# A fused attention and mixture-of-experts kernel: the order of the slots' scatters, the place of one flag product, and the engine that writes the last tile

## The chip, the core and the metric

The kernel runs on one core of one Trainium2 chip. The metric is device time in microseconds (us): the median of the runs of one launch. TensorE is written PE here, with PEld for its weight loads; DVE is VectorE, ACT is ScalarE, POOL is GpSimd, SP is the queue that issues most transfers.

## The reference: what is computed

Windowed attention over q, k and v of shape 4 x 8 x 768 x 64 (batch, heads, tokens, width), then a router and eight experts over the 3072 rows of 512 that the attention gives:

```python
scores = scale * np.matmul(q, k.transpose(0, 1, 3, 2))
rel = pos[:, None] - pos[None, :]
is_global = pos[None, :] < int(n_global)
is_local = (rel >= 0) & (rel < int(n_local))
...
a = np.exp(scores)
a = a / (np.sum(a, axis=-1, keepdims=True) + 1e-09)
...
xn = x / (np.linalg.norm(x, axis=-1, keepdims=True) + 1e-06)
en = expert_emb / (np.linalg.norm(expert_emb, axis=-1, keepdims=True) + 1e-06)
logits = xn @ en.T / tau
expert_idx = np.argmax(logits, axis=1)
...
for e in range(E):
    mask = expert_idx == e
    h = np.maximum(x[mask] @ w1[e], 0.0)
    out[mask] = gate_w[mask, None] * (h @ w2[e])
```

With n_global = 8 and n_local = 96 each token attends to 96 tokens behind it and to the first eight. An expert multiplies its tokens by a 512 x 1024 and a 1024 x 512 matrix, all in float32.

## The kernel before, in words

**Attention** (`window_attention`, L377) works in 32 steps over groups of four heads, the first 24 for three batches one after the other and the last eight for the fourth. A step scores two blocks of 96 queries (`score`, L480), exponentiates them on ACT (`grow`, L486), multiplies them by a table of weights on DVE (`weigh`, L493), and multiplies the blocks of the step before by v (`attend`, L509 and L519). In the same steps the halves of a batch that are finished go through routing (`half_turns`, `half_router`): turning (L582, L550, L568), the division by the softmax sums on DVE (`store_x`, L591) with the square sum on ACT (L596), and the generator `choose` (L192), which is advanced one piece at a time. For the last two batches a half has three row blocks, and its router comes in the third turn (`hf.count` is 2); for the others a whole batch is chosen, one turn later.

`choose` gives each token its expert and its slot in a list in memory. Its pieces: the highest score and its expert on DVE (L203 to L211); then, when it is sent a bank, counting products on PE (L217, L220) and the root, a power on POOL (L224); then the new counts on DVE (L228, L230); then the scale of the logits from the root (DVE L234 to L236), the exponential (ACT L237) and the slot (L246). Each block's `scatter` (a reciprocal on DVE, L256, and an indirect DMA that POOL issues, L257) is put on the list `k.later`. `scatter_later` (L296) takes one, two or three blocks off it in each step (L789); the DMA is told to wait for the step's last score product (`scored`). All scatters must have landed before the first expert's slots are read (L976), and then its first 256 rows are gathered (L986) and run through its first matrix while attention ends (L663, L671).

**The experts** (L1688 to L1742). For each, tokens are gathered by POOL, turned, and multiplied by the first matrix by a seven-product scheme (`first_by_seven`, L1296 and L1308) in one of several arms of a Switch, each for a number of tokens. The second matrix takes whole tiles (L1229, L1231) and odd parts (L1242, L1244) in the arm, and the first two tiles by another seven-product scheme, `Pair` (L1085): sums of the weights and of the hidden values on DVE (L1040 to L1043, L1065 to L1068), products on PE (L1102), copies and scalings on ACT (L1128, L1132, L1139, L1154), sums on DVE (L1107, L1114). `Pair.fourth` writes a quarter of the first tile through ACT (L1148). `Pair.end` writes the last quarter in `rest` (L1160), which is issued in the next expert, or at the end of the program for the last one. The scatters of finished rows are issued by POOL (L1248).

**Flags.** `good` holds whether all softmax sums are in range (`check_sums`, L607), `fits` whether the two numbers fit the window. `flag_leftover` (L1514), issued inside expert 2 on the list `ahead`, multiplies the two (L1519, DVE), adds over partitions with a one-column product (L1520, PE) and makes a flag (L1521 to L1528). The program's end branches on it (L1542) to a slow path that isn't taken here.

**What sets the order.** In attention, PE, ACT, DVE and SP run in the order in which the program names the instructions; POOL's order there is chosen by the framework's scheduler. In the experts all five engines run in program order.

Of the kernel before, what the change touches and what calls it, by code (L numbers as in the profile page):

```python
# [12 lines left out]
ALU = mybir.AluOpType  # L13
# [282 lines left out]
def scatter_later(k, n, behind=None):  # L296

    for scatter, t in k.later[:n]:
        scatter(t, behind)
    del k.later[:n]  # L300
# [76 lines left out]
def window_attention(k, ctx):  # L377
# [375 lines left out]
    waiting, active = [], []  # L753
    weights = [(0, i) for i in range(PIECES)]
    for s, (g, p) in enumerate(steps):
        if s % 8 == 0:
            before = t if s else None
            pair = groups[s // 4 : s // 4 + 2]
            t = new_batch(g.b)
            t.groups = pair  # L760
            for x in pair:
                x.batch = t
        ahead = s // 4 + 2
        if ahead < len(groups):
            if s % 4 == 0:
                open_group(groups[ahead])
            load_part(groups[ahead], s % 4)
        if s == len(steps) - 5:
            early.close()
            k.w.append(new_weights(k, k.second_weights()))  # L770
            weights.extend((1, i) for i in range(PIECES))

        def weights_part(n=1):
            for _ in range(n):
                if s >= 11 and weights:
                    e, i = weights.pop(0)
                    load_weights_part(k, e, k.w[e], i)

        if s == 5:
            nc.sync.dma_start(k.x_dram[k.ZR : k.ZR + 1, :].rearrange("o (p c) -> (o p) c", p=P), k.zrow[:])  # L780
            empty_slots(k)

        us = g.units[2 * p : 2 * p + 2]
        for u in us:
            scored = score(u)
        grow(us[0], 0)
        grow(us[0], 1)
        weigh(us[0])
        scatter_later(k, 1 if s < len(steps) - 8 else 2 if s < len(steps) - 3 else 3, scored)  # L789
        grow(us[1], 0)  # L790
        todo = [(x.pairs[a], i) for x, a, i in turns[s]]
        if todo:
            turn(*todo.pop(0))
        grow(us[1], 1)
        for x in todo:
            turn(*x)
        if s == 2:
            next(table)
        if 1 <= s <= 3:
            emb.send(bank() if s == 3 else None)  # L800
        if waiting and (s >= 8 * (B - 1) or all(hf.phase >= 3 for hf in active)):
            active.append(start_half(*waiting.pop(0)))
        if s == len(steps) - 1:
            weigh(us[1])
        for hf in active:
            half_turns(hf)
        if s == len(steps) - 1:
            first_gathers()
        ready = s > 8 * (B - 1) - 2 and steps[s - 1][0].m == 1 and steps[s - 1][1] % 2
        if s < len(steps) - 1 and not ready:  # L810
            weigh(us[1])
        weights_part()
        for hf in active:
            if hf.router and hf.phase == hf.count:
                next(hf.router)
        if s > 0:
            q, qp = steps[s - 1]
            attend(q, qp, s < len(steps) - 10)
            if q.m == 1 and qp % 2:
                waiting.append((prev, qp // 2))  # L820
        if ready:
            weigh(us[1])
        for hf in active:
            if hf.phase == 0:
                score_experts(hf, bank())
            half_router(hf)
            hf.phase += 1
        active = [hf for hf in active if hf.phase < (hf.count + 2 if hf.router else 3)]
        if s == len(steps) - 3:
            scatter_later(k, len(k.later))  # L830
            first_rows()
        weights_part()
        prev = t
# [24 lines left out]
    scatter_later(k, len(k.later))  # L858
    check_sums(before)
    check_sums(t)  # L860
    for f in range(1, k.NF):
        first_product(f)

# [221 lines left out]
class Pair:  # L1085


    def __init__(self, k, rows, a, left, w2, sums):
        self.k, self.ids, self.a, self.left, self.sums = k, rows[1], a, left, sums
        self.gate = [rows[0][:, i, 2:3] for i in range(2)]  # L1090
        self.b = [[w2[:, 4 * i : 4 * i + 4, j * 256 : (j + 1) * 256] for j in range(2)] for i in range(2)]
        tmp = k.tp.tile([P, 5, 256], F32, name="ptmp", tag="ptmp")
        self.p1, self.p5, self.u2, self.u3, self.u3g = (tmp[:, i] for i in range(5))
        self.u2g = k.late.tile([P, 256], F32, name="u2g", tag="u2g")[:]
        self.y = [k.yp.tile([P, k.DM], F32, name="y", tag="y") for _ in range(2)]
# [49 lines left out]

    def fourth(self):
        self.product(self.m, self.a[0][1], self.b[1][0], True)
        self.k.nc.scalar.mul(self.part(0, 0), self.m, self.gate[0])  # L1148

    def end(self, ps):  # L1150

# [187 lines left out]
def expert(k, now, coming, widths, unfinished):  # L1339


    tc = k.tc
    w1, w2 = now.w
    hT = new_hidden(k)
    if coming:
        coming.xT = new_turned(k)

    def between(f):
        at = {1: (0,), 2: (1,), 3: (2,), 4: (3,)} if now.e else {5: (0,), 6: (1, 2), 7: (3,)}
        for j in at.get(f, ()) if coming else ():  # L1350
            turn_row(k, coming.rows, coming.xT, j, k.nc.scalar.copy)

    a = [[hT[:, 4 * j : 4 * j + 4, i * P : (i + 1) * P] for j in range(2)] for i in range(2)]
    now.sums, spare = weight_sums(k, w2)
    left, making = hidden_sums(k, a)
    more, ahead = [], []
    if coming:
        coming.token_sums, more = token_sums(k, coming.xT)
        if now.e:
            coming.first_sums, ahead = first_sums(k, coming.w[0])  # L1360
    spare = [spare[:2], spare[2:], ahead[:1], ahead[1:2], more[:2], []]
    if now.e == 1:
        spare[2:6] = [], ahead[:1], ahead[1:2] + more[:1], more[1:2]
    tiles = range(2 if now.e else 1, CAP // P)
    ps = None if now.e else k.work0.tile([P, k.DM], F32, name="work", tag="work")
    k.order = list(range(4, 8)) + list(range(4)) if now.e else list(range(8))
    steps = widths_of(now.e)
    for arm in tc.Switch(now.width.index, len(steps), hint=now.width.hint):
        w = steps[arm]
        if now.e:  # L1370
            first_by_seven(k, now, hT, w, between, list(spare))
            for make in making:
                make()
        else:
            first_by_eight(k, now.xT, w1, hT, w, between)
        for size in (32, 64):
            if w % (2 * size) >= size:
                part_in_arm(k, now, hT, w2, w // (2 * size) * 2 * size, size)
        for j in tiles:
            if j < w // P:  # L1380
                second_in_arm(k, now, hT, w2, j)
        if ps:
            second(k, ps, hT, w2, range(k.NF // 2))

    def scatters():
        for j in tiles:
            scatter_rows(k, now.y[:, j - 1, :], now.tile_ids[:, j : j + 1])
        for size in (64, 32):
            scatter_rows(k, now.y_part[size][:], now.parts[size][0], P // size)

    def choose_next():
        if coming:
            give_hint(k, coming.e, widths[coming.e])

    out = [scatters]
    if now.e:
        pair = Pair(k, now.rows, a, left, w2, now.sums)
        choose_next()
        out += unfinished.pop()()
        number = [lambda: widths.append(take_width(k, now.e + 2))] if now.e + 2 < k.E else []  # L1400
        if now.e == k.E - 2:
            number.append(lambda: load_flag(k))
        if now.e == 2:
            ahead.append(lambda: flag_leftover(k))
        pair.begin(spare=(more[2:], number + ahead[2:3], ahead[3:]))
        ps = k.work0.tile([P, k.DM], F32, name="work", tag="work")
        unfinished.append(pair.end(ps[:, 0:256]))
        out.append(pair.scatter(1))
    else:
        choose_next()  # L1410
        widths.append(take_width(k, 2))
        out += unfinished.pop()()
        for make in more:
            make()
        second(k, ps, hT, w2, range(k.NF // 2, k.NF))
        unfinished.append(lambda: end_second(k, now.rows, ps))
    return out
# [96 lines left out]
def flag_leftover(k):  # L1514

    nc = k.nc
    k.flags = flags = k.const.tile([P, 2], F32, name="flags")
    ps = k.work.tile([P, 512], F32, name="work", tag="work")
    nc.vector.tensor_tensor(out=k.good[:], in0=k.good[:], in1=k.fits[:], op=ALU.mult)  # L1519
    nc.tensor.matmul(ps[:, 0:1], lhsT=k.ones[:], rhs=k.good[:], start=True, stop=True)  # L1520
    nc.vector.tensor_scalar(out=flags[:, 0:1], in0=ps[:, 0:1], scalar1=float(P), scalar2=None,  # L1521
                            op0=ALU.is_lt)
# [251 lines left out]
```

## Time and profile before

| what | value |
|---|---|
| median of 3 runs | 529.67 us (523.33 to 529.82) |
| the profiled execution's own time | 530.46 us |
| its span, first to last instruction | 528.70 us |
| mean granted clock of PE | 0.988 |
| PE busy | 504.3 us (95%) |
| PEld busy | 415.2 us (79%) |
| DVE busy | 302.6 us (57%) |
| ACT busy | 198.0 us (37%) |
| POOL busy | 151.1 us (29%) |
| moved by DMA | 76.32 MB, 144 GB/s in the mean |

A line of the timeline gives the start and the duration in us, the engine, the line of the kernel, the operation, the tile written and the tiles read, and in brackets how long the engine stood idle before it and what ended that. A row of the stages gives a stretch, the busy time of PE, PEld, DVE, ACT and POOL in it with the number of instructions, the granted clock of PE as a share, the busy share of the DMA engines, and GB/s. In the 40-slice rows each digit is a tenth.

### The profile page before, as it was taken

The numbers are of one execution on the slowest core, as the hardware profiler recorded it, in microseconds if no ns is written. First come the engines' busy times: TensorE is split into PE (matmuls) and PEld (weight loads), VectorE is DVE, ScalarE is ACT, GpSimd is POOL, SyncE is SP. The second block draws the span as 40 slices with busy tenths as digits, with TensorE's granted clock in tenths as the row PEclk, the third lists the DMA queues.
The fourth block names the chain that finished last, engine by engine and source line by source line (L and its number), as shares of the span: only waits on it lengthen the run. The fifth ranks groups of instructions, "written<-read, shape, count | busy, mean of one in ns | idle before, by whom it ended". The sixth has DMA issues, their size and how long they took to land. (4 is left out here: it accounts for less than half of the span.)

```text
span 528.7 us, 13699 instructions
## 1 busy us (share of the span) xinstructions
PE 504.3 (95%) x5606; PEld 415.2 (79%) x5606; DVE 302.6 (57%) x601; ACT 198.0 (37%) x494; POOL 151.1 (29%) x169
## 2 busy tenths in 40 slices
PE   8999999999988999999989998999999999999995
PEld 7777787877765787859878757989989789859964
DVE  5646677766784573755745605675746645615531
ACT  4867766767654321302312312322322222312211
POOL 4222121151453234354240013344053050013022
PEclk9999999999998799999999999999999999999999
DMA  8989998999533234827683016548056064001001
GB/s 161 203 184 177 233 231 184 217 218 215 103 102 112 90 83 97 261 65 263 215 283 125 1 37 230 217 148 282 28 207 246 3 221 163 1 12 69 0 22 66
DMA packets 111421, 76.32 MB, mean 144 GB/s; under 512 B 87077, under 2 KB 95269, under 8 KB 111281
## 3 DMA queue, kind: packets, MB, share of 16 engines
q1 hardware_dynamic: 102769, 59.00, 42.6%
q0 software_dynamic: 6912, 15.26, 8.7%
q8 instruction: 63, 1.03, 0.9%
q14 instruction: 77, 0.63, 0.4%
q10 hardware_dynamic: 1600, 0.39, 0.3%
HBM read 61.66 MB, written 17.16 MB: 149 GB/s over the span
## 5 line engine op out<-in xcount | busy, mean ns | idle before, releaser
L493 DVE TENSOR_TENSOR ex<-ex,table 126x768 f32<-126x768 f32 x64 | 61.2, 961 | 44.9 <-ACT ex L486 44.0
L1308 DVE TENSOR_TENSOR hT<-big,hT 128x320 f32<-128x320 f32 (+4 forms) x70 | 39.4, 566 | 49.8 <-PE big L1296 48.4
L1248 POOL DMA_INDIRECT out_dram<-y_arm,tids x17 | 17.1, 1004 | 168.0 <-ACT y_arm L1231 121.7
L486 ACT ACTIVATE ex<-pa 126x384 f32<-126x384 f32 (+1 forms) x128 | 53.4, 476 | 21.9 <-PE pa L480 19.7
L1296 PE MATMUL big<-xT,w1t 128*128 128x160 f32 (+4 forms) x336 | 59.4, 330 | 1.7 <-issue 1.7
L1296 PEld LDWEIGHTS big<-xT,w1t 128*128 128x128 f32 x336 | 54.2, 190 | 4.4 <-issue 2.5
L509 PE MATMUL od<-ex,v 126*64 126x192 f32 (+1 forms) x576 | 49.8, 322 | 0.0
L986 POOL DMA_INDIRECT xg<-x_dram,idss x32 | 33.9, 1058 | 44.6 <-PE big L1296 22.9
L509 PEld LDWEIGHTS od<-ex,v 126*64 126x64 f32 x576 | 36.9, 145 | 8.6 <-issue 3.7
L480 PE MATMUL pa<-qT,kT 64*32 64x128 f32 (+3 forms) x2048 | 40.6, 268 | 2.6 <-issue 2.4
L480 PEld LDWEIGHTS pa<-qT,kT 64*32 64x32 f32 (+1 forms) x2048 | 30.9, 107 | 14.8 <-issue 11.9
L257 POOL DMA_INDIRECT meta<-mt,slot x24 | 27.7, 1154 | 44.9 <-DVE rd L553 21.1
L1296 PE MATMUL big<-xsum,fsum 128*128 128x160 f32 (+4 forms) x224 | 39.6, 330 | 0.0
L1015 ACT COPY xT<-work 128x256 f32<-128x256 f32 x56 | 18.0, 376 | 56.7 <-PE work L1012 55.3
L1296 PEld LDWEIGHTS big<-xsum,fsum 128*128 128x128 f32 x224 | 36.1, 190 | 1.1
L1229 PE MATMUL work<-w2t,hT 128*128 128x512 f32 x80 | 35.1, 593 | 0.0
L1102 PE MATMUL big<-wsum,hsum 128*128 128x256 f32 x136 | 31.1, 380 | 1.0 <-issue 0.5
L430 POOL COPY v<-v 30x896 f32<-30x896 f32 (+1 forms) x15 | 17.8, 1197 | 49.0 <-DMA v<-in_v_dram 29.4
L1310 ACT ACTIVATE hT<-hT 128x320 f32<-128x320 f32 (+4 forms) x42 | 21.6, 533 | 25.5 <-DVE hT L1308 25.3
L1102 PEld LDWEIGHTS big<-wsum,hsum 128*128 128x128 f32 x136 | 25.7, 190 | 5.6 <-issue 1.3
L1229 PEld LDWEIGHTS work<-w2t,hT 128*128 128x128 f32 x80 | 15.1, 190 | 17.7 <-issue 17.6
L1107 DVE TENSOR_TENSOR ptmp<-big,ptmp 128x256 f32<-128x256 f32 x16 | 6.7, 421 | 37.0 <-ACT ptmp L1128 17.0
(245 smaller groups left out, 903.0 us busy)
## 6 DMA issues: line engine op xcount, KB each, us to landing
w1t<-in_moe_w_dram SPq DMA_DIRECT2D x6, 2048.0 KB
w2t<-in_moe_w_dram SPq DMA_DIRECT2D x6, 2048.0 KB
v<-in_v_dram SPq DMA_DIRECT2D x32, 192.0 KB
x_dram<-xs SPq DMA_DIRECT2D x23, 256.0 KB
k<-in_k_dram SPq DMA_DIRECT2D x28, 192.0 KB
q<-in_q_dram SPq DMA_DIRECT2D x28, 192.0 KB
w1t<-in_moe_w_dram SPq DMA_DIRECT2D x32, 128.0 KB
w2t<-in_moe_w_dram SPq DMA_DIRECT2D x32, 128.0 KB
```

The lines of the kernel that those rows point to most:

```text
L257: i = nc.gpsimd.indirect_dma_start(out=k.meta[:], out_offset=bass.IndirectOffsetOnAxis(ap=slot[:, t : t + 1], axis=0), in_=mt[:, t, :], in ...
L480: i = nc.tensor.matmul(u.sp[e][k0:k1, a * n + c0 : a * n + c1], lhsT=t.kT[rows, j, k0:k1], rhs=t.qT[rows, j * BLK + c0 : j * BLK + c1], st ...
L486: nc.scalar.activation(u.ex[:, e], u.sp[e][0:ROWS, 0 : 2 * u.n].rearrange("p (a c) -> p a c", a=2), AF.Exp, scale=k.scale)
L493: nc.vector.tensor_tensor(out=exv, in0=exv, in1=tab[:, :, 0 : u.n // BLK, :], op=ALU.mult)
L509: nc.tensor.matmul(g.od[a][e * D : (e + 1) * D, at : at + c1 - c0], lhsT=g.v[0:ROWS, 2 * a + e, u.j, :], rhs=u.ex[:, e, a, c0:c1], start=f ...
L986: i = k.nc.gpsimd.indirect_dma_start(out=xg[:], out_offset=None, in_=k.x_dram[0 : upto or k.N + 1, :], in_offset=bass.IndirectOffsetOnAxis ...
L1015: copy(out=xT[:, :, a, j * half : (j + 1) * half].rearrange("p c (q i) -> p c q i", i=LACE), in_=laced(ps[:])[:, a])
L1102: i = self.k.nc.tensor.matmul(ps, lhsT=x[:, f, :], rhs=w[:, f, :], start=f == 0 and not add, stop=True, skip_group_check=True)
L1229: nc.tensor.matmul(ps[:], lhsT=hT[:, f, j * P : (j + 1) * P], rhs=w2[:, f, :], start=i == 0, stop=i == k.NF - 1)
L1296: nc.tensor.matmul(to[f // 2][:, f % 2 * 256 : f % 2 * 256 + h], lhsT=x[:, l, f * P : (f + 1) * P], rhs=y[:, l, 0:h], start=not (add or f ...
L1308: nc.vector.tensor_tensor(out=to, in0=x, in1=z, op=ALU.add)
L1310: nc.scalar.activation(to, to, AF.Relu)
```

## The change

Three places change. In a step in which a router is about to reach its root (a half in `active` whose phase is its count), the step's scatters are issued behind the halves' turns, and with that behind the root; in every other step they stay where they were. The product of `good` and `fits` moves from `flag_leftover` to the end of `window_attention`. And `Pair` learns whether it belongs to the last expert; if so, `fourth` scales its quarter tile on DVE.

```diff
+        due = 1 if s < len(steps) - 8 else 2 if s < len(steps) - 3 else 3
+        if not any(hf.router and hf.phase == hf.count for hf in active):
+            scatter_later(k, due, scored)
+            due = 0
-        scatter_later(k, 1 if s < len(steps) - 8 else 2 if s < len(steps) - 3 else 3, scored)
         grow(us[1], 0)
...
         for hf in active:
             half_turns(hf)
+        scatter_later(k, due, scored)
...
     check_sums(before)
     check_sums(t)
+    nc.vector.tensor_tensor(out=k.good[:], in0=k.good[:], in1=k.fits[:], op=ALU.mult)
     for f in range(1, k.NF):
         first_product(f)
...
-    def __init__(self, k, rows, a, left, w2, sums):
+    def __init__(self, k, rows, a, left, w2, sums, final=False):
+        self.final = final
...
     def fourth(self):
         self.product(self.m, self.a[0][1], self.b[1][0], True)
-        self.k.nc.scalar.mul(self.part(0, 0), self.m, self.gate[0])
+        scale = self.k.nc.vector.tensor_scalar_mul if self.final else self.k.nc.scalar.mul
+        scale(self.part(0, 0), self.m, self.gate[0])
...
-        pair = Pair(k, now.rows, a, left, w2, now.sums)
+        pair = Pair(k, now.rows, a, left, w2, now.sums, not coming)
...
     ps = k.work.tile([P, 512], F32, name="work", tag="work")
-    nc.vector.tensor_tensor(out=k.good[:], in0=k.good[:], in1=k.fits[:], op=ALU.mult)
     nc.tensor.matmul(ps[:, 0:1], lhsT=k.ones[:], rhs=k.good[:], start=True, stop=True)
```

## The prediction

> **What bounds the kernel now.** I read the page first (busy shares, clock row), then who waits for whom on TensorE from 200 us on, then the order of time round the three places that the change touches, then the clock by stage, and last the end. In the page, PE is busy for 504.3 of 528.7 us: time is won only where PE stands idle, where its clock is low, or behind its last matmul.
>
> ```profile
> PEclk9999999999998799999999999999999999999999
> ```
>
> Here the reader is to see that the clock is low in two of the 40 slices only, 159 to 185 us, the end of attention. By stage (PE, PEld, DVE, ACT, POOL busy, then the clock):
>
> ```profile
> 157.00:161.00 4.00, 3.91 (x31) 2.52 (x35) 2.92 (x12) 1.58 (x6) 1.40 (x3) 0.63 0.17 57
> ...
> 172.00:176.00 4.00, 4.00 (x30) 3.31 (x32) 2.38 (x9) 0.76 (x3) 0.89 (x1) 0.50 0.41 118
> ```
>
> With 161 to 165 (0.94) and 176 to 180 (0.69), the clock lost is 4 x (0.37 + 0.06 + 0.50 + 0.31) = 4.96 us. Ahead of the first stretch PE stands still for 1.68 us. GpSimd's order there:
>
> ```profile
> 145.57 0.92 POOL L224 TENSOR_TENSOR ss<-ss,half 128x3 f32<-128x3 f32 x1
> 146.69 1.27 POOL L257 DMA_INDIRECT meta<-mt,slot  x1 [0.20 <-PE pa L480]
> 150.88 1.56 POOL L257 DMA_INDIRECT meta<-mt,slot  x1 [2.91 <-PE pa L480]
> 152.74 1.40 POOL L257 DMA_INDIRECT meta<-mt,slot  x1 [0.31 <-issue]
> 154.16 1.61 POOL L224 TENSOR_TENSOR ss<-ss,half 128x3 f32<-128x3 f32 x1
> ```
>
> The power (L224, the router's root) of the step that PE begins at 145.34 has its sums at 151.55 (ScalarE's accumulator read, 151.37 + 0.18) and starts at 154.16, behind two scatters. What hangs on it:
>
> ```profile
> 155.81 0.17 DVE L234 TENSOR_SCALAR ss<-ss 128x3 f32<-128x3 f32 x1 [0.78 <-POOL ss L224]
> ...
> 156.44 0.22 ACT L237 ACTIVATE lg<-lg 128x24 f32<-128x24 f32 x1 [2.61 <-DVE lg L236]
> ...
> 157.09 0.55 PE L550 MATMUL pa<-ident,den 128*128 128x128 f32 x3 [1.68 <-ACT ex L486]
> ```
>
> ScalarE's exponentials stand in its queue behind L237, and PE needs a bank that they free: late power, late VectorE, late ScalarE, PE idle. From 200 us on PE's one long wait is the flags' product:
>
> ```profile
> 320.56 1.22 DVE L1068 TENSOR_TENSOR fsum<-w1t,fsum 128x1024 f32<-128x1024 f32 x1
> 321.70 0.15 DVE L1519 TENSOR_TENSOR good<-good,fits 128x1 f32<-128x1 f32 x1
> 321.90 0.30 PEld L1520 LDWEIGHTS work<-good,ones 128*128 128x128 f32 x2 [2.24 <-DVE good L1519]
> 321.90 0.38 PE L1520 MATMUL work<-good,ones 128*128 128x1 f32 x2 [1.83 <-DVE good L1519]
> ```
>
> A one-column product waits behind two long sums on VectorE, and PE with it, 320.07 to 321.90. And the end:
>
> ```profile
> 519.69 0.43 DVE L1107 TENSOR_TENSOR y<-ptmp 128x256 f32<-128x256 f32 x1 [1.69 <-ACT ptmp L1154]
> 520.39 0.98 POOL L1248 DMA_INDIRECT out_dram<-y,idss  x1 [2.93 <-DVE y L1107]
> ...
> 522.63 0.48 DVE L1114 SCALAR_TENSOR_TENSOR y<-work,mts,u2g 128x256 f32<-128x256 f32 x1 [2.52 <-PE work L1102]
> 523.89 0.98 POOL L1248 DMA_INDIRECT out_dram<-y,idss  x1 [2.52 <-ACTq L1542]
> ```
>
> The scatter before the last starts 0.27 us behind VectorE's write (520.12); the last one 0.78 us behind (523.11).
>
> **The change part by part.**
>
> *Flags.* L1519 leaves the middle of expert 2. As built, it stands between the third and fourth sum of w2 at routing's end (near 194.9). It is 0.15 us there; VectorE next sits idle for 4.51 us (before L1066), which covers it, and without that cover it would cost 0.16. PE's 1.83 us go. What is late next: as built, the matmul behind L1520 (L1102, work from wsum and hsum) now carries a VectorE wait of its own, since L1520's wait no longer covers it. That tile's last reader is L1114 at 303.73, done at 304.21, so it waits for nothing; if it were the L1114 at 320.16 (done at 320.64) 0.6 would stay, if L1068, all but 0.1. Expert 3's first matmuls also get VectorE waits; the latest is L1068, done at 321.78, and PE gets there at 327.41 - 1.83 = 325.6. The gain is kept, as PE is busy for 50.00 of 50 us in each stage from 350 to 500 and loads and gathers are released by PE's own progress. Taken: -1.83, ends -1.83 and -0.1.
>
> *Last tile.* L1148 moves from ScalarE (0.47 at 520.91) to VectorE, which is idle from 520.12 to 522.63. Nearest rows: 0.43 for L1107 and 0.75 for L1030's 128x512 product, so it ends by 521.7. Behind it on that queue only the last write waits, and that for PE. The final scatter loses its ScalarE wait; as built it keeps one DMA and one VectorE wait, like the scatter at 520.39. By that row it starts at 523.11 + 0.27 = 523.38: -0.51. Ends: 0 (the 0.78 is not the wait's) and -0.78.
>
> *Scatters.* Only two steps change in the built order, those that PE begins at 133.84 and 145.34. In the third late root's step nothing is left to scatter. No engine does more. In both, the reciprocals (0.22 the pair) go behind VectorE's L591 (0.67).
>
> First step: GpSimd's copy of v, which stood behind two scatters and waited for them to land (144.55 to 145.48, 3.88 idle), now goes ahead of them. So does the power, which waits only for ScalarE's sum (138.52): it starts near 138.6 instead of 145.57. Nobody waited for this power: its reader L234 (147.42) found VectorE busy without a gap. But the copy at 144.55 fell on VectorE's L204, which took 0.80 against 0.18 in the later halves. With the copy gone, VectorE is 0.62 earlier, and PE's wait of 0.51 at 147.56 (for L530) goes. The two scatters start near 140.4 and 141.7 instead of 137.86 and 139.15; the next on the queue is not ready before 142.76, so none queue up. GpSimd's copy and power now meet VectorE's weighing at 136 to 140; at worst it loses 0.9 + 0.9, against 1.74 of idle before 141.88.
>
> Second step: **the built GpSimd order does not change.** Both scatters still stand ahead of the power, since no list fixes GpSimd's order here. What moves is VectorE: reciprocals 0.67 later behind L591, 0.62 earlier through L204, so ready at 150.2 as now; scatters at 150.9 and about 152.3, and the power no earlier than 153.7. The weighings that overlap it are about 0.6 earlier. PE thus wins 0.5 and gives back most of it in the same stall. Ends: -1.8 (both scatters at 0.96 and the power at 0.89, the shortest rows: 150.88 + 0.96 + 0.30 + 0.96 + 0.89 = 154.0 for 155.77) and +0.67 (no L204 gain). Taken: -0.4, between them but nearer today's order, which is what was built.
>
> [...]
>
> **Sum.** -1.83 - 0.51 - 0.4 = -2.74. The profiled execution took 530.46 (span 528.70): 527.7. The median of the runs shown is 529.67, 0.79 below: 526.9, said as 527.0. The clock's two low stretches are taken as they are.
>
> The clock is the doubt. [...] Here it falls behind 1.68 us. [...]
>
> **Rivals.**
> 1. *The low clock stays away* (L204's relief closes PE's 0.51 gap, or the stall shrinks). For: one run of before took 523.33, 6.34 under the median, and the stretches are worth 4.96. Against: the change leaves the stall and the second stretch's causes. 527.0 - 5.0 = 522.0; with the whole 6.34, 520.7.
> 2. *Slower: a later power holds the clock down.* VectorE doesn't get its 0.62 back, the second step's scatters and power come 0.67 later, PE idles 2.3 us, and the clock stays at half from 157 until 172. Price: 11 us at half are 5.5 of clock, less the 0.24 lost there already, so 5.3. 529.67 - 2.34 + 0.67 + 5.3 = 533.3. It decides from 1.67 us of lost clock on. Against: the clock came back by 165 today.
> 3. *The flags' wait is only replaced* by L1102's new one, on L1068: -0.1 instead of -1.83, so 528.7. Against: the reader at 303.73.
> 4. *The scatters' part does nothing at all*, as in the second step's unchanged order: 529.67 - 2.34 = 527.3, inside the first case.
>
> **How the numbers follow.** Forecast with rival 4: 0.62, range of its own 525.3 (all lower ends) to 529.1 (-1.23 with 0.6 of the flags' wait left, 0 for the last tile, +0.67). Rival 1: 0.19. Rival 2: 0.11. Rival 3: 0.08. The range 520.5 to 531.0 takes in the first, second and fourth of these and leaves rival 2 and some tails out. Over or under 2% (10.6 us, about what a measurement of this kernel can tell from no change): below 519.1 needs rival 1 with every lower end, 0.02; above 540.3 nothing worked out here reaches, 0.01; within: 0.97.
>
> **What would show it.** Right: PE's wait before the flags' matmul is gone and the matmul behind it follows at once; the last scatter starts about 0.27 behind VectorE; GpSimd's first late power near 139 and L204 back at 0.18; the second power still behind two scatters and PE still idle 1.5 to 2.3 us behind it; low clock near 157 and 172. Wrong: a clock row without a dip (rival 1), or with one long dip (rival 2); a wait of L1102 on VectorE near 321.8 (rival 3); a last scatter still 0.78 behind.

## The result, and the profile after

| | before | after |
|---|---|---|
| median of 20 runs each, us | 526.12 (522.91 to 529.82) | 523.67 (521.68 to 529.42) |
| ratio, 95% interval | | 0.9961 [0.9938, 0.9984] |
| profiled execution's own time, us | 530.46 | 524.56 |
| its span, us | 528.70 | 522.8 |
| PE busy, us | 504.3 | 500.1 |

The ratio is a gain of 2.05 us (0.84 to 3.26), inside 2%. The prediction said -2.74. Its absolute figure, 527.0, lies 3.3 above the new median, since the three runs it stood on had a median of 529.67 and twenty runs of the same kernel have 526.12. The two profiled executions lie 5.9 us apart, more than the medians do. Of that, 2.0 us were won before the first late root's step begins (131.83 for 133.84), in a stretch in which PE, ACT, DVE and POOL run the same instructions in the same order in both: a single pair of profiles can't be subtracted to a microsecond.

Lines move with the change: the flags' product L1519 is now L865, its matmul L1520 is L1526, L1102 is L1108, L1068 is L1073, L1114 is L1120, L1148 is L1155, L1248 is L1255. The lines of attention keep their numbers.

**Flags.** From the order of time of the changed kernel round the flags' matmul:

```profile
316.10 0.28 PE L1526 MATMUL work<-good,ones 128*128 128x1 f32 x2
...
316.24 1.97 PE L1108 MATMUL work<-wsum,hsum 128*128 128x256 f32 x8
316.76 1.22 DVE L1073 TENSOR_TENSOR fsum<-w1t,fsum 128x1024 f32<-128x1024 f32 x1
```

There is no bracket behind L1526: PE did not wait. Nor did the matmul behind it, which reads while the long sum L1073 still runs. The 1.83 us are gone, and nothing took their place.

**The end.** The last writes of the changed kernel:

```profile
515.55 0.48 DVE L1155 TENSOR_SCALAR y<-big,mts 128x256 f32<-128x256 f32 x1 [0.80 <-PE big L1108]
517.28 0.48 DVE L1120 SCALAR_TENSOR_TENSOR y<-work,mts,u2g 128x256 f32<-128x256 f32 x1 [1.24 <-PE work L1108]
518.04 0.98 POOL L1255 DMA_INDIRECT out_dram<-y,idss  x1 [2.03 <-DVE y L1120]
```

VectorE's last write ends at 517.76 and the scatter starts 0.28 behind it, where it was 0.78 behind.

**The two late roots.** GpSimd's order in the changed kernel:

```profile
136.53 0.88 POOL L224 TENSOR_TENSOR ss<-ss,half 128x3 f32<-128x3 f32 x1 [0.77 <-ACT fhT L596]
137.83 1.05 POOL L257 DMA_INDIRECT meta<-mt,slot  x1 [0.41 <-issue]
139.18 0.96 POOL L257 DMA_INDIRECT meta<-mt,slot  x1 [0.30 <-issue]
...
151.78 1.27 POOL L257 DMA_INDIRECT meta<-mt,slot  x1 [0.31 <-issue]
153.08 0.89 POOL L224 TENSOR_TENSOR ss<-ss,half 128x3 f32<-128x3 f32 x1
```

The first power is ahead of its step's scatters, and the second is still behind them, as built. But the second ends at 153.97 instead of 155.77. What hangs on it, in order of time:

```profile
153.98 0.95 DVE L493 TENSOR_TENSOR ex<-ex,table 126x768 f32<-126x768 f32 x1
...
154.85 0.16 DVE L234 TENSOR_SCALAR ss<-ss 128x3 f32<-128x3 f32 x1
...
156.13 0.55 PE L550 MATMUL pa<-ident,den 128*128 128x128 f32 x3 [1.18 <-ACT ex L486]
```

L234 no longer waits for POOL: it stands behind the weighing L493 on VectorE. PE's stall is 1.18 for 1.68.

**What was given back.** The step behind the first late root begins with 64 score products on PE. Before:

```profile
139.99 1.44 PE L480 MATMUL pa<-qT,kT 64*32 64x128 f32 x64
...
145.34 1.13 PE L480 MATMUL pa<-qT,kT 64*32 64x128 f32 x64
```

After, the same two groups:

```profile
137.97 0.87 PE L480 MATMUL pa<-qT,kT 64*32 64x128 f32 x40
139.11 0.43 PE L480 MATMUL pa<-qT,kT 64*32 64x128 f32 x5 [0.27 <-issue]
139.84 0.44 PE L480 MATMUL pa<-qT,kT 64*30 64x96 f32 x5 [0.29 <-issue]
140.59 0.48 PE L480 MATMUL pa<-qT,kT 64*32 64x128 f32 x14 [0.31 <-issue]
...
144.99 1.13 PE L480 MATMUL pa<-qT,kT 64*32 64x128 f32 x64
```

The group that took 1.44 us takes 3.10 (137.97 to 141.07), broken up by pauses of some 0.3 us that no wait explains (the profile calls such time "issue"). The step, from one group's start to the next, takes 7.02 us for 5.35. What is new beside it are the two moved scatters: they start 0.14 before and 1.21 behind the group's start, and before the change they started 2.13 and 0.84 ahead of it. The prediction did not price this.

**The clock.** The page's row has one dip where before had a longer one:

```profile
PEclk9999999999998999999999999999999999999999
```

In stretches of 1 us (PE, PEld, DVE, ACT, POOL busy, then the clock) of the changed kernel:

```profile
160.00:161.00 1.00, 0.47 (x9) 0.17 (x6) 0.00 (x0) 0.00 (x0) 0.69 (x2) 1.00 0.61 178
161.00:162.00 1.00, 0.54 (x9) 0.33 (x9) 0.00 (x0) 0.00 (x0) 0.83 (x1) 1.00 0.20 51
162.00:163.00 1.00, 0.68 (x16) 0.31 (x12) 0.00 (x0) 0.36 (x1) 0.00 (x0) 1.00 0.05 9
163.00:164.00 1.00, 1.00 (x8) 0.87 (x7) 0.46 (x1) 1.00 (x4) 0.00 (x0) 0.71 0.01 3
```

The dip follows 3 us in which PE is about half busy (0.47, 0.54 and 0.68), and those 3 us are again a score group broken up beside three scatters (159.17 to 163.00).

### The profile page after: what moved, and what is told of

Same layout as the page of the kernel before. It is cut to its first block, busy times and chain, and to the rows that moved or that the text cites. A ratio compares the mean times of both kernels' runs of the same rounds, so it can differ in the third digit from the quotient of the medians.

```text
span 522.8 us, 13699 instructions
## 1 busy us (share of the span) xinstructions
PE 500.1 (96%) x5606; PEld 411.3 (79%) x5606; DVE 301.8 (58%) x602; ACT 197.2 (38%) x493; POOL 153.7 (29%) x169
## 4 chain that ended last, share of the span: by engine, by line
PE 67%; issue 18%; DVE 3%; POOL 3%; ACT 3%; DMA 3%; SPq 1%; POOLq 1%; ACTq 0%; DVEq 0%
PE big L1303 17%; PE big L1108 9%; PE od L509 7%; PE pa L480 5%; PE work L1236 4%; PE od L519 3%; PE pa L455 3%; PE work L1108 3%; PE work L1249 3%; PE pa L671 2%; PE work L1017 2%; POOL out_dram L1255 2%; PE big L1279 2%; PE pa L582 2%; PE work L1027 1%
## 5 line engine op out<-in xcount | busy, mean ns | idle before, releaser
L493 DVE TENSOR_TENSOR ex<-ex,table 126x768 f32<-126x768 f32 x64 | 61.3, 964 | 45.1 <-ACT ex L486 44.9
L1255 POOL DMA_INDIRECT out_dram<-y_arm,tids x17 | 17.1, 1004 | 167.4 <-ACT y_arm L1238 121.1
L991 POOL DMA_INDIRECT xg<-x_dram,idss x32 | 35.4, 1106 | 42.9 <-PE big L1303 21.5
L509 PE MATMUL od<-ex,v 126*64 126x192 f32 (+1 forms) x576 | 47.0, 309 | 0.0
L480 PE MATMUL pa<-qT,kT 64*32 64x128 f32 (+4 forms) x2048 | 41.0, 263 | 3.7 <-issue 3.5
L509 PEld LDWEIGHTS od<-ex,v 126*64 126x64 f32 x576 | 35.3, 139 | 7.9 <-issue 3.8
L1108 PE MATMUL big<-wsum,hsum 128*128 128x256 f32 x136 | 31.1, 380 | 1.1 <-issue 0.6
L1108 PEld LDWEIGHTS big<-wsum,hsum 128*128 128x128 f32 x136 | 25.7, 190 | 5.6 <-issue 1.4
```

Of the source, the lines that this page charges most:

```text
L480: i = nc.tensor.matmul(u.sp[e][k0:k1, a * n + c0 : a * n + c1], lhsT=t.kT[rows, j, k0:k1], rhs=t.qT[rows, j * BLK + c0 : j * BLK + c1], st ...
L493: nc.vector.tensor_tensor(out=exv, in0=exv, in1=tab[:, :, 0 : u.n // BLK, :], op=ALU.mult)
L509: nc.tensor.matmul(g.od[a][e * D : (e + 1) * D, at : at + c1 - c0], lhsT=g.v[0:ROWS, 2 * a + e, u.j, :], rhs=u.ex[:, e, a, c0:c1], start=f ...
L991: i = k.nc.gpsimd.indirect_dma_start(out=xg[:], out_offset=None, in_=k.x_dram[0 : upto or k.N + 1, :], in_offset=bass.IndirectOffsetOnAxis ...
L1108: i = self.k.nc.tensor.matmul(ps, lhsT=x[:, f, :], rhs=w[:, f, :], start=f == 0 and not add, stop=True, skip_group_check=True)
L1255: i = k.nc.gpsimd.indirect_dma_start(out=k.out.rearrange("t (i m) -> (t i) m", i=n), out_offset=bass.IndirectOffsetOnAxis(ap=ids, axis=0), ...
```

## The experiments

Theory at the start: the flags and the last tile give what the sum said, and the scatters' new order gives back part of it, because its scatters fall on the next step's score products. Rivals: all three parts gain; or the flags' gain is lost later, and the scatters give the rest. Each set of four has runs of the kernel before beside it: e1 to e4 (528.29 us, 35 runs), e5 to e8 (529.34, 32 runs), e9 to e12 (527.37, 27 runs).

### e1, e2, e3: one part alone

e1 keeps the flags' move, e2 the last tile, e3 the scatters' order; the other two are as before. The whole edit of e1 against before:

```diff
     check_sums(t)
+    nc.vector.tensor_tensor(out=k.good[:], in0=k.good[:], in1=k.fits[:], op=ALU.mult)
...
-    nc.vector.tensor_tensor(out=k.good[:], in0=k.good[:], in1=k.fits[:], op=ALU.mult)
```

> The kernel before, with the flags' product alone moved to routing's end. Theory: PE's wait of 1.83 us ahead of the one-column product goes whole (0 to 0.1 left), the next product follows at once, and the median falls by about 1.8 us, of 526. Rival: the next product's own wait on VectorE takes its place (1.2 to 1.8 us of it left), and the time is the same within 0.6. Both: attention and the last scatter (0.78 behind VectorE's write) as before.

> The kernel before, with the last expert's quarter tile alone scaled by VectorE. Theory: the last scatter starts 0.27 to 0.30 us behind VectorE's last write instead of 0.78, and from that write to the end of the span it is 0.5 shorter; the median falls by 0.5, less than the spread of the runs. Rival: the 0.78 belongs to VectorE's last write or to the branch at the end, and stays at 0.7 to 0.8. Both: PE's wait of 1.8 at the flags stays.

> The kernel before, with the scatters' order alone changed. Theory: the maximum's subtraction on VectorE in the step of the second late root falls from 0.80 to 0.18 us since no copy of v falls on it, PE's wait of 0.5 for the sums' copy in that step goes, and from the first score of that step to the turn of the sums two steps on it is 0.5 to 0.7 shorter than the 11.75 of before (11.1 to 11.3). Median lower by 0.4 to 0.6. Rival: it does nothing, 11.7 again and the median the same. In both the second power stands behind two scatters, and PE still idles for 1.0 to 2.0 us ahead of the turn of the sums.

| kernel | median us | ratio to before | in us of 528.29 |
|---|---|---|---|
| e1, flags | 525.27 | 0.9956 [0.9923, 0.9988] | -2.3 |
| e2, last tile | 528.23 | 1.0013 [0.9981, 1.0045] | +0.7 |
| e3, scatters | 529.70 | 1.0036 [1.0002, 1.0071] | +1.9 |

The flags' part is faster by itself. In e2's trace the last scatter starts 0.28 behind VectorE (519.61 to 519.89) and in e1's, without that part, 0.77 (518.94 to 519.71), but half a microsecond can't be read from an interval of 1.7 us to either side. The scatters' part is slower by itself, by 0.1 to 3.8 us. The rival that it gains falls. In e3's trace the stretch that was to be shorter is so: from the second late root's step to the turn of the sums (L550) it takes 11.19 us, for 11.75 before. The loss must lie elsewhere.

### e4: the root ahead of the scatters in both steps

The changed kernel, in which a root step's scatters also depend on that step's power, so that POOL's order is forced in the second step too.

```diff
-    nc.gpsimd.tensor_tensor(out=ss, in0=ss, in1=k.half[:, 0:n], op=ALU.pow)
+    k.root = nc.gpsimd.tensor_tensor(out=ss, in0=ss, in1=k.half[:, 0:n], op=ALU.pow).ins
...
-            wait_for(k, i, [behind])
+            wait_for(k, i, [behind] + ([root] if root else []))
...
-        scatter_later(k, due, scored)
+        scatter_later(k, due, scored, due and k.root)
```

> The changed kernel, with the scatters of a root's step made to wait for that step's power, so that the second late power stands ahead of its two scatters on GpSimd. It then starts near 151 instead of 153 (counted as in the changed kernel's profile). If scatters ahead of the power set PE's idle time there (1.18 us in the changed kernel), that falls to 0.5 or less and the median by 0.7. If VectorE's own queue sets it by now (the scale's first instruction started as the weighing ahead of it ended), PE idles for 1.0 to 1.3 us as before and the median doesn't move. A third case: the scatters, now later, meet the weighings and the scale's reader waits for nothing, but the slots' landing is late: the ids' cast would start over 0.5 later behind the last scatter.

525.87 us, ratio 0.9991 [0.9956, 1.0026]; the ratio of the medians alone is 0.9954, so its time tells little. The second power starts at 151.44 instead of 153.08 and PE no longer waits before L550. It is no faster for it than the change: scatters now start at -0.77, +0.94 and +2.21 us from the start of the next score group, and that takes 4.20 us with four pauses. The wait was removed, and in its place stands a broken score group.

### e5: the scale of the logits later

The changed kernel, in which the last piece of the second late half's router stands behind the next step's exponentials, so that ScalarE's queue no longer holds them back.

```diff
-            next(hf.router)
+            if (hf.t.b, hf.h) == (B - 2, 1):
+                k.scale_later = hf.router
+            else:
+                next(hf.router)
...
+        if s == len(steps) - 3:
+            next(k.scale_later)
```

> The changed kernel, with the last piece of that router (scale, exponential, slot) moved from the end of one step to behind the next step's exponentials. If the wait of 1.0 to 1.3 us ahead of the turn of the sums comes from the exponential of the logits standing in ScalarE's queue ahead of that step's exponentials, it goes (0.3 or less), and the median falls by about 1 us against the changed kernel. If VectorE's weighing or the banks hold PE there anyway, 0.8 or more stays. Both: the ids' cast starts up to 2 us later, which costs nothing, as the first gathered rows are turned 10 us behind their gathers.

529.39 us, 1.0016 [0.9982, 1.0050]. PE's wait before L550 is gone here too, and the kernel has lost the change's whole gain. The mean granted clock of its runs is 0.988, where that of the changed kernel's is 0.997, so a part of the loss goes with the clock; what lowers it was not tested. The time did not follow this one stall of PE.

### e6: scatters kept for the next step

The changed kernel, with the scatters of the root steps put off to the step after, and the final ones one step later.

```diff
-            scatter_later(k, due, scored)
-            due = 0
+            scatter_later(k, due + kept, scored)
+            due = kept = 0
...
-        scatter_later(k, due, scored)
+        kept += due
...
-        if s == len(steps) - 3:
-            scatter_later(k, len(k.later))
+        if s == len(steps) - 2:
```

> The changed kernel, with no scatter issued ahead of a score group of the late steps: a root's step keeps its scatters for the next step, behind that step's scores, and the flush of the last ones comes one step later, behind its scores, as does the load of the first slots. Theory (found in the traces): a score group, dense in instructions, stands still in pieces of 0.3 us ('issue') when GpSimd's indirect DMAs run beside it. Then the step behind the first late root lasts 5.3 to 5.6 us from score to score, as before the change, not 7.0; the three late score groups last 1.1 to 1.4 instead of 2.0 to 3.9; and the median falls by 2 to 4 us against the changed kernel. Rival: the pieces belong to places in the instruction stream or to the weights' loads, and stay: same time within 1.

530.13 us, 1.0023 [0.9997, 1.0049]. The group behind the first late root has no scatter near it, takes 1.13 us, and its step 5.03. The scatters that were kept start at 144.33, 145.68 and 146.95, and now the group at 145.87 takes 3.67 with three pauses. The pauses moved with the scatters. The mean granted clock of its runs is low too (0.990).

### e7, e12 and e8: without the scatters' part, and the change again

e7 is the changed kernel with the scatters' order of before; e12 is e7 once more; e8 is the changed kernel once more.

```diff
-        due = 1 if s < len(steps) - 8 else 2 if s < len(steps) - 3 else 3
-        if not any(hf.router and hf.phase == hf.count for hf in active):
-            scatter_later(k, due, scored)
-            due = 0
+        scatter_later(k, 1 if s < len(steps) - 8 else 2 if s < len(steps) - 3 else 3, scored)
...
-        scatter_later(k, due, scored)
```

> The kernel before, with the flags' product and the last tile changed, and the scatters' order as before. If the scatters' new order costs (alone it took 1.0036 of before's time, and the step behind the first late root lasts 7.0 us instead of 5.3), this is faster than the changed kernel by 0.5 to 2 us, near 0.995 of before. If that order gains its 0.4 as predicted, it is slower than the changed kernel by that, and the step lasts as long in both.

> The changed kernel once more, beside the others on one chip: a median 2 us below before's by both theories, with the same wait of 1.2 us ahead of the turn of the sums. Of its traces: the step behind the first late root lasts about 7.0 us from score to score if the scatters' new place causes it, and anything from 5.3 to 7.3 if chance does.

> The flags' product and the last tile alone, with the scatters in their old order, once more beside the two kernels with half of the scatters' order, for a firmer interval. If the scatters' new order costs time, 0.990 to 0.995 of the kernel before, as the 0.992 measured first; if that first run was luck, 0.9965, as the whole change.

| kernel | median us | ratio to before |
|---|---|---|
| e7, flags and last tile | 525.24 | 0.9920 [0.9884, 0.9956] |
| e12, the same | 524.40 | 0.9936 [0.9911, 0.9962] |
| the change | 523.67 | 0.9961 [0.9938, 0.9984] |
| e8, the change again | 526.94 | 0.9968 [0.9937, 1.0000] |

The mean of the first two is 0.9928, of the last two 0.9965. The difference, 0.0037, is 1.9 us; with half widths of 0.0022 and 0.0020 (root of the sum of squares, halved) it is uncertain by 0.0029. So the scatters' order costs 1.9 us, 0.4 to 3.5, the same as e3 found by itself. e7 has the lowest ratio of all that was run: it beats the kernel before, and by this comparison the changed one (e10 below can't be told from it).

### e9, e10, e11: which scatters

e9 has the new order in the second late root's step alone, e10 in the first alone (`- 5` for `- 7`):

```diff
-        if not any(hf.router and hf.phase == hf.count for hf in active):
+        if s == len(steps) - 7 or not any(hf.router and hf.phase == hf.count for hf in active):
```

e11 is the changed kernel without the first step's two scatters:

```diff
+        if s == len(steps) - 7:
+            del k.later[:due]
+            due = 0
         scatter_later(k, due, scored)
```

> The changed kernel with the scatters' new order only in the second late root's step (the one that PE begins near 144); in the first one the two scatters are issued early, as before the change. Theory A (the two moved scatters of the first late root's step, running beside the next step's score products, stall them): the step behind that root, from its first score product to the next step's, takes 5.3 to 6.3 us instead of 7.0 to 8.8, and the kernel is at least as fast as with the flags and the last tile alone: ratio to the kernel before about 0.992. Rival B (the stall comes with the earlier power and copy of v, or with the second root's order): still 7 us or more there, ratio about 0.9965, as the changed kernel.

> The changed kernel with the scatters' new order only in the first late root's step; in the second one they are issued early, as before the change. Theory A: the step behind the first root takes 7.0 to 8.8 us, and the kernel is no faster than the whole change, ratio about 0.9965 to 0.999. Rival B (second root's order is what costs): 0.992, like the flags and the last tile alone.

> The changed kernel without the two scatters of the first late root's step: 256 tokens never reach an expert's list, so their rows of the result stay unfilled; the counts, and with them the experts' matrix products, are the same. Theory A (the two DMAs in flight stall the next step's score products): the step behind that root falls from 7.0 to about 5.3 us, its score products follow one another without the gaps of 0.3 us that end with an issue, and ScalarE has no 2 us wait there. Rival B (the place in the order, not the DMAs): 7 us or more again.

e9: 524.74 us, 0.9956 [0.9930, 0.9982]. e10: 524.83 us, 0.9940 [0.9913, 0.9967]. Both lie between the whole change and none of it, neither is told from either, and e10, which was to keep the cost, is if anything the faster. So the theory that the first step's order alone is what costs falls. The profile of e10 shows why. In order of time:

```profile
138.40 1.13 PE L480 MATMUL pa<-qT,kT 64*32 64x128 f32 x64
...
140.92 1.05 POOL L257 DMA_INDIRECT meta<-mt,slot  x1 [0.20 <-issue]
142.28 0.96 POOL L257 DMA_INDIRECT meta<-mt,slot  x1 [0.30 <-DVE lg L574]
143.44 0.55 PE L480 MATMUL pa<-qT,kT 64*32 64x128 f32 x5
143.54 0.95 POOL L257 DMA_INDIRECT meta<-mt,slot  x1 [0.30 <-issue]
144.43 0.41 PE L480 MATMUL pa<-qT,kT 64*32 64x128 f32 x4 [0.44 <-issue]
...
```

GpSimd's copies of v ran 2.54 us in that execution, so the scatters came 2.5 us behind the group's start and missed it; the next group was hit instead. The order of issue doesn't say which group is hit: the time of the scatters does. e9's profiled execution, with a span of 529.8, is the slowest of its twelve; in it the old order of the first step hit the group too (scatters at -0.37 and +0.92, 2.91 us, the step 6.82).

e11, with two scatters left out, has the group whole:

```profile
138.78 1.13 PE L480 MATMUL pa<-qT,kT 64*32 64x128 f32 x64
...
143.81 1.13 PE L480 MATMUL pa<-qT,kT 64*32 64x128 f32 x64
```

The step takes 5.03 us, with the power and the copies of v ahead as in the changed kernel (the power starts at 138.24). Without the two DMAs there is no pause: they, and not the places in the order, are what the score products meet. (Its one time, 521.95, is not used, since it leaves 256 tokens out.)

### All score groups together

Over the 14 profiles, every group of 64 score products from 100 us on, by the number of scatters that start between 1.0 us before and 1.75 us after its start:

| scatters | groups | median length us | shortest to longest |
|---|---|---|---|
| 0 | 111 | 1.13 | 1.12 to 3.48 |
| 1 | 39 | 1.4 | 1.12 to 3.35 |
| 2 | 22 | 2.9 | 1.61 to 4.90 |
| 3 | 8 | 3.9 | 3.81 to 4.13 |

Of the 111 groups without a scatter, 97 take at most 1.24 us. Five of the longer ones are the last group of attention, and beside them run the first gathers of the experts (L986 in the kernel before), which are indirect DMAs from GpSimd too: the five take 1.57 to 3.48 us, with a gather that starts between 1.14 before and 0.74 behind their start. In seven other profiles the first gather starts 0.88 to 1.24 us behind, and the last group takes 1.13. So it is not the scatters alone. The bounds of the count were drawn after seeing the profiles, and some lengths hold half a clock, but the steps from 0 to 3 are far larger than that.

From the first late root's step on, without the last group, the sum of what the groups took over 1.13 each was, with the old order, 1.7 (before), 5.5 (e1), 1.9 (e2), 4.8 (e7) and 4.1 (e12), 3.6 in the mean; with the new order 5.4 (after), 6.1 (e3) and 4.0 (e8), 5.2 in the mean. The difference of 1.6 has the sign and the size of the measured cost, but the two sets overlap.

The score groups are not all of it. In e8 the group behind the first late root is whole (139.71, 1.13 us), the moved scatters start 0.97 and 2.33 us behind its start, and then ScalarE stands still, and PE behind it:

```profile
143.52 0.49 ACT L486 ACTIVATE ex<-pa 126x384 f32<-126x384 f32 x1 [2.18 <-remote]
...
144.06 0.55 PE L568 MATMUL pa<-ident,fhT 128*128 128x128 f32 x3 [1.99 <-ACT ex L486]
```

The step as a whole, from the start of that group to the start of the next, and ScalarE's longest wait before an exponential in it:

| scatters of the first late root's step | profiles | step, us | ScalarE's wait, us |
|---|---|---|---|
| left out or put off | e6, e11 | 5.03, 5.03 | 0.14, 0.14 |
| new order | after, e3, e4, e5, e8 | 7.02, 7.07, 7.29, 7.08, 8.84 | 2.12 to 2.23 |
| new order, scatters 2.5 us late | e10 | 5.04 | 0.14 |
| old order | before, e1, e2, e7, e9, e12 | 5.35, 5.82, 5.29, 6.32, 6.82, 6.43 | 0.31 to 1.64 |

(e8's 8.84 holds 3.4 us at half clock.) The six of the new order have a mean of 7.06 and the six of the old one of 6.00, so the step costs 1.1 us more in the new order, and the old order costs up to 1.8 as well. The rest of the 1.9 is not located, the less so as the second late root's step gains.

## Why the prediction was right, and where it was wrong

**Flags: right.** The term was -1.83. The wait is gone, the matmul behind carries no new one, and e1 alone gives -2.3 us (-4.1 to -0.6). Rival 3 falls: the bank's last reader was the earlier one, as worked out.

**Last tile: right in the trace.** The term was -0.51; the scatter's distance went from 0.78 to 0.28. No time resolves it by itself. The two parts together are -3.8 us by e7 and e12 (0.9928 of 527), more than the -2.34 of their terms.

**Scatters: wrong, in sign.** The step that failed is "Taken: -0.4, between them but nearer today's order", with ends of -1.8 and +0.67; measured, the part costs +1.9, outside both. Rival 4, that it does nothing, falls with it. What it said of waits came true or better. On the scale of before (2.01 later) the first power starts at 138.54, said near 138.6. L204 took 0.18, and PE's 0.51 before L530's reader is gone. The second power came earlier than "no earlier than 153.7": 153.08, or 153.43 on the scale of its own step, and its end, 153.97 or 154.32, is near the lower end of the range, 154.0. PE's stall of 1.18 is below the 1.5 to 2.3 said, so the second step gained more than the prediction dared to take (11.14 for 11.75 us from its start to L550). But the 0.62 of L204 was the luck of one profile and not the old order's price: L204 took 0.80 in before and 0.46 in e1, and 0.18 in e2, e7, e9 and e12, all with the old order in the first step. PE's wait at L217 was 0.51 in before, 0.96 and 0.41 in e1 and e2, and none in e7, e9 and e12.

The failing sentence is "the next on the queue is not ready before 142.76, so none queue up". It looked at the moved scatters' own queue and at VectorE, found them free, and priced the scatters' new neighbours at nothing. PE's next score group begins in that very place, and ScalarE's exponentials behind it; the step took 7.02 us for 5.35. In before's own profile the price could be read: its group at 161.76, with one scatter 0.08 behind its start, took 2.32 us, and its group at 145.34, with none there until 1.35, took 1.13.

```profile
161.76 1.40 PE L480 MATMUL pa<-qT,kT 64*32 64x128 f32 x42
161.84 0.96 POOL L257 DMA_INDIRECT meta<-mt,slot  x1 [0.30 <-issue]
...
163.47 0.61 PE L480 MATMUL pa<-qT,kT 64*32 64x128 f32 x22 [0.31 <-issue]
```

**The sum.** -2.74 was said and -2.05 measured, by two errors that cancel: the flags and the last tile give 1.5 more than their terms, the scatters 2.3 less. That the sum came so near is luck. The absolute 3.3 us is the base, as said above.

For the 1.5 the granted clock gives a likely cause. The prediction took the two low stretches of before's profile, near the end of attention, as they are, and looked for the clock at no other place; but it fell behind the flags' wait too, in two of the three profiles that have it (before, e2, e3). In e2, whose lines are L1522 and L1103 here, it looks like this:

```profile
316.27 0.38 PE L1522 MATMUL work<-good,ones 128*128 128x1 f32 x2 [1.83 <-DVE good L1521]
316.51 2.42 PE L1103 MATMUL work<-wsum,hsum 128*128 128x256 f32 x8
```

The eight products behind it took 1.97 us in before and after, and 2.42 here; the granted clock was 0.50 from 318 to 320 us. In e3 they took 3.25, with 0.50 from 320 to 322. Each of the two lost 1.7 us of clock time there, and before's own profile none. The eleven profiles without the wait lost none between 300 and 340 us. The mean granted clock of the runs goes the same way: 0.992 to 0.994 in the kernel before, 0.991 and 0.993 in e2 and e3, and 0.995 to 0.997 in the change and in e1, e4, e7 to e10 and e12. The difference of about 0.003 is worth 1.0 us by the slope given under the clock, and 1.6 us if the whole span is counted, both estimates. No run varied the clock alone, and e5 and e6 are low without the wait, so this is a reading and not a test; the intervals (2 us and more for a part) allow that some of the 1.5 is chance.

**The clock.** The stretches near 157 and 172 were to stay; there is one, at 163 to 167. In stretches of 2 us from the first late root's step to the end of attention, the clock time lost was 5.12 us in before's profile and 1.70 in after's, and over the others 0.00 (e3, e4, e10, e11, e12), 1.70 (e1, e2, e7, e8, e9) and 3.4 (e5, e6). e7 and e12 are the same kernel and have 1.70 and 0.00, so at the end of attention the change doesn't turn rival 1 on or off: one execution draws it and another does not. Within a kernel, a run's time falls by 3.4 us for each 0.01 of mean clock (214 runs of e1 to e12 and of before beside them, r = -0.57): about a third of the variance that all these intervals carry.

The losses come in units of 1.70 us, and one of them is 3.4 us at a granted clock of 0.50 (in the rows of 1 us above, from about 163.4 to 166.8). What brings one on is not shown. The prediction put it behind PE's stall of 1.68 us, but the dip after 163 follows 3 us in which PE was busy for 0.47, 0.54 and 0.68, with no pause of PE above 0.36. From the first late root's step to the end of attention, nine of the 14 profiles have 11 such falls (none in e3, e4, e10, e11 and e12), and in the 3.4 us ahead of each PE was busy for 0.7 to 2.4 us. Such a stretch doesn't always bring a fall: in e3 PE was busy for 0.59, 0.35 and 0.55 from 162 to 165, and the granted clock was 1.00 until 169.

**Open.** What the scatters take from PE and ScalarE is not settled. PE's pauses have no semaphore behind them; ScalarE's wait is named "remote" and lasts 2.12 to 2.23 us in the five profiles where the moved scatters meet its exponentials. The scatters move little data: in the changed kernel three of them moved 96 packets and under 0.01 MB from 136 to 146 us. Yet beside indirect DMAs that GpSimd issues the table above has groups of 3.9 for 1.13 us, and e11 takes the pauses away with the DMAs. Whether it is the DMAs in flight, their issue or GpSimd's own work was not separated. Nor was it tried to issue the scatters from a fixed time behind the score group, which the readings suggest.

## What to carry to other kernels

When an instruction is moved to fill one engine's wait, list what runs beside its new place on every engine, not only what queues behind it: the two scatters were free on their own queue, and their new place cost the kernel some 1.9 us. A part whose price is a matter of when two streams meet shows differently from one execution to the next (with the old order the step took 5.29 to 6.82 us in six profiles), so it is settled by medians of the part alone, and a pair of profiles tells only which neighbours to look at. Take the base from as many runs as can be had: three runs put it 3.5 us off, more than the whole change.

## What the runs showed of the hardware

- A group of 64 score products (1.13 us) took 1.4, 2.9 or 3.9 us in the median with one, two or three of GpSimd's indirect scatters starting beside it, in pauses of about 0.3 us that show no wait. With a gather that GpSimd issues beside it, the last group of attention took 1.57 to 3.48 us in five profiles, and ScalarE stood still for 2.12 to 2.23 us beside the moved scatters in another five (after, e3, e4, e5, e8).
- The last scatter started 0.78 and 0.77 us behind VectorE's last write where ScalarE had written a part of its tile (before, e1), and 0.28 where it had not (after, e2). Whether the number of waits or the end of ScalarE's own queue (L1542, which the profile names there) makes the difference was not separated.
- From the first late root's step to the end of attention the clock's losses came as 0, 1.70, 3.4 and 5.1 us, for code that is nearly the same (e7 and e12, one kernel: 1.70 and 0.00). Ahead of the 11 falls there, PE had been busy for 0.7 to 2.4 of 3.4 us; in e3 a stretch with 1.49 in 3 us had none behind it.
- VectorE's L204, with a copy on GpSimd beside it, took 0.80 us (before), and 0.18 without one beside it (after).
